# Twenty-six products in the last two groups: a negation leaves ScalarE, a raw quarter is derived by a sum, and the slab ring has eleven places

## The chip, the core and the metric

The kernel runs on one core of a Trainium2 chip. Its time is the device time of one execution in microseconds (us). A core has five engines that run beside each other, each with its own instructions in a fixed order: TensorE (PE; its weight loads are PEld) multiplies, VectorE (DVE), ScalarE (ACT) and GpSimd (POOL) work elementwise, and SyncE (SP) issues most transfers. A transfer that SP issues (SPq in the profile) waits in SP's order for what it depends on; everything behind it on SP waits too.

## The reference

Attention within chunks of 64 tokens is followed by a Fourier mix and a two-layer network, all in float32:

```python
# q, k, v: (8, 8, 576, 64); each chunk of 64 tokens attends to itself
attn = softmax(q_c @ k_c.T / sqrt(64)); x = (attn @ v_c)      # x: (8, 576, 512)
mixed = real(fft(fft(x, axis=1), axis=2))
u = x + mixed
un = (u - mean(u)) / sqrt(var(u) + 1e-6)                      # over the last axis
out = u + relu(un @ w_ch1) @ w_ch2                            # w_ch1: 512 x 2048, w_ch2: 2048 x 512
```

The change concerns the last product, with w_ch2, for the last two of nine groups of tokens.

## The kernel before, in words

**Groups and stages.** The tokens are cut into tiles of 128 and these into nine groups of four tiles (`groups`; eight groups of one batch entry each, and one of what is left of all). Each group passes an up stage (`un @ w_ch1` and relu, result `h1`) and a down stage (`h1 @ w_ch2` and the sum with u). While a group is multiplied, the attention and the Fourier mix of the next are done in between (`sides`), for the last groups no more. The generator `mlp(g)` yields after each small piece of TensorE work, and the loop at the end of the kernel hands out the other engines' work at each step `t`. The order on each engine is the order in which the Python code issues the instructions: nothing is rearranged.

**Fewer products.** From group 2 on the up stage (`up_halves`, L1271) and from group 1 on the down stage (`down_halves`, L1322) use seven half-size products in place of eight. For the last two groups (`FEW = NG - 2`, that is groups 7 and 8) the down stage is `down_few` (L1386): w_ch2 is seen as eight blocks b11 to b42, `h1` as sixteen blocks a11 to a44, and 26 products of sums of such blocks (`PRODUCTS`) give the result. A row of `PRODUCTS` names the left operand, the block on the right, a PSUM half (`c`, `b`, `d`, `f`, upper case for the second half), where the product is added with which sign (`+31` is block row 3, column 1), and the sums of `h1` blocks that GpSimd makes afterwards (`sums`, L1172). `EARLY` lists six such sums that are issued within the up stage of the same group, between products 15 and 20 of its 28.

**Blocks of w_ch2.** The right-hand blocks that are sums are made once, by `make_rest`, on GpSimd (L1122): `MADE` lists them, those whose name begins with s are stored in DRAM (`s3`, L1129). This is done in two halves of 512 columns each (`for half in range(2)`). A half first loads eight raw blocks from DRAM (`s2`, L1109), then makes 23 results: 22 on GpSimd, and `s18=-h` on ScalarE (L1118). They live in a list of 14 spare buffers of 128x512, taken from its front and given back at its end when the last reader has been issued; a buffer that is stored from is given back when the store has been issued, and the next writer waits for the store to land. A store is issued when three more stored blocks have been made after it. make_rest starts within the down stage of group 6 and is spread over the steps; at step `begin[FEW] + 2 * HF - 3`, late in the up stage of group 7, what is left of it is issued.

**The raw quarters.** w_ch2 as halves has four quarters. `keep2_whole` (L1079) and `keep2` (L1071) write three raw quarters and four sums to DRAM early in the program, for the seven products; `keep2_last` (L1083) writes the fourth raw quarter, the right half of the top rows (blocks b12 and b22), which only make_rest and the 26 products read.

**Slabs.** The right-hand operands come through rings of slabs in SBUF, filled by `fetch`: `fetch(1)` for the up stage (256 KB each, ten places, L1144, into `wa`), `fetch(2)` for seven-product down stages (1 MB, three places, L1149, into `wb`), `fetch(3)` for the 26 products (512 KB, six places, L1147, into `wb`). After each product one more slab is asked for, and waits for its place to be free. The first six `fetch(3)` are issued at the step named above, right after the rest of make_rest.

**Outputs.** `store` writes a finished tile: L1027 on SP for tiles of one kind, L1036 on SP and ScalarE for another, L1030 to L1032 for the last group. L1027 writes 128 KB in the shape 2x32x512.

**ScalarE in the up stage.** In each pair of the up stage, ScalarE copies a product from PSUM (L1276), which VectorE and later TensorE steps wait for, and applies relu (L1285, L1288, L1291). `s18=-h` stands between these.

Of the kernel before, what the change touches and what calls it, by code (L numbers as in the profile page):

```python
# [8 lines left out]
FP32 = mybir.dt.float32  # L9
# [7 lines left out]
def kernel(  # L17
# [32 lines left out]
    nc = tc.nc  # L50
    B, H, S, D = q.shape
    DM = H * D
# [8 lines left out]
    KF = DFF // 128  # L61
    HM, HQ = DM // 2, DM // 4
# [4 lines left out]
    G = 2 * NM  # L67
# [4 lines left out]
    one_p = ctx.enter_context(tc.tile_pool(name="one", bufs=1))  # L72
# [6 lines left out]
    dram = ctx.enter_context(tc.tile_pool(name="dram", bufs=1, space=bass.MemoryType.DRAM))  # L79
# [23 lines left out]
    NO, HF = 7, KF // 2  # L103
    UP = (1, 0, 2, 3, 4, 6, 5)
    s1 = dram.tile([HF // 2, NO, 128, 2 * 2 * 128], FP32, name="s1")
    s2 = dram.tile([NO + 1, 128, HF * HM], FP32, name="s2")
    NS1, NS2, Z1, Z2 = 10, 3, 2 * 2 * 128, HF * HM
    slab1 = [wa[:, i * Z1:(i + 1) * Z1].rearrange("p (k r f) -> p k r f", r=2, k=2) for i in range(NS1)]
    slab2 = [wb[:, i * Z2:(i + 1) * Z2].rearrange("p (m e) -> p m e", m=HF) for i in range(NS2)]
# [9 lines left out]
    NH, Z3 = 2, 4 * HM  # L119
# [1 line left out]
        ("a41", "b11", "c", "+41", "a41=a22+a42 a22=a21-a22 a21=a41-a21"),  # L121
        ("a44", "b42", "b", "+42", "a44=a24+a44 a31=a21+a31"),
        ("y0", "s8", "d", "+12", ""),
        ("y3", "s21", "c", "+31+32+42", "y3=y3+a43"),
        ("y1", "s0", "d", "+11+21", "y1=a44-y1 y1=y1-a23 y0=a12-y0"),
        ("a22", "b22", "f", "-22", "a22=a32-a34 a32=a42-a32"),
        ("a23", "s19", "d", "+22", ""),
        ("a44", "s15", "b", "+41", ""),
        ("a31", "s10", "f", "+32", "a31=a42-a22 a13=a13+a14 a24=a24+a31 a14=a14+a34 a34=a13+a34 y2=a34+y2"),
        ("y1", "s3", "b", "-21-22", ""),  # L130
        ("y3", "b32", "f", "+42", "a43=a44+a43 a12=a41-a12 a12=a12+a13 y0=y0-a32"),
        ("a22", "b21", "C", "+31", ""),
# [9 lines left out]
        ("a14", "s6", "D", "", ""),  # L142
        ("y2", "s18", "F", "-32", ""),
        ("a12", "b21", "B", "-11", ""),
        ("y0", "b22", "D", "+12", ""),
        ("a33", "s23", "F", "-31", ""),
    )
    EARLY = "y0=a11-a13 a11=a11-a21 y1=y0-a21 y2=a31-a41 a31=a33-a31 y3=y2-a33"
    MADE = (
        "u=b41-b31", "s3=b31-b41", "s15=u-b42", "s7=u-b11", "s8=b12+b22", "s0=u-s8", "t=b32-b42", "s19=u+t",  # L150
        "v=b32-b31", "s10=b11-b12", "s23=v-s10", "s21=s10-b32", "s24=s10-b22", "w=b22-b21", "s22=w-s10",
        "s4=b42-b41", "s25=w+s4", "s1=b21-s4", "s17=b21+b41", "h=b12+b32", "s12=h-s17", "s6=b42-h", "s18=-h",
    )
    STORED = tuple(text.split("=")[0] for text in MADE if text[0] == "s")
    NR2, NS3 = len(PRODUCTS), 6
    s3 = dram.tile([len(STORED), 128, Z3], FP32, name="s3")
    slab3 = [wb[:, i * Z3:(i + 1) * Z3].rearrange("p (m e) -> p m e", m=4) for i in range(NS3)]

    def parsed(text):

        out_, rest = text.split("=")
        sub = "-" in rest
        a, b = rest.split("-" if sub else "+")
        return out_, a, b, ALU.subtract if sub else ALU.add
# [913 lines left out]
        for o, m0, e0 in ((0, m, 0), (4, HF + m, 0), (5, HF + m, HM)):  # L1078
            nc.sync.dma_start(out=to[o, :, m:m + 2], in_=w2[:, m0:m0 + 2, e0:e0 + HM])  # L1079

    def keep2_last(i):
        to = s2.rearrange("o p (m e) -> o p m e", m=HF)
        nc.sync.dma_start(out=to[NO, :, 2 * i:2 * i + 2], in_=w2[:, 2 * i:2 * i + 2, HM:DM])  # L1083

    def block_of(name):

        if name[0] == "s":
            return s3[STORED.index(name)]
        k, j = int(name[1]) - 1, int(name[2]) - 1
        o = ((0, NO), (4, 5))[k // 2][j]  # L1090
        return s2[o, :, k % 2 * Z3:(k % 2 + 1) * Z3]

    def make_rest():

        z, spare = Z3 // 2, []
        for i in range(4):
            spare.append(xall[:, 2 * G:2 * G + 4, :].rearrange("p a f -> p (a f)")[:, i * z:(i + 1) * z])
        for tag, n in (("q", 2), ("k", 2), ("zf", 2), ("two", 1), ("qT", 1), ("kT", 1), ("pT", 1)):  # L1100
            t = one_p.tile([128, n * z], FP32, tag=tag, name="part")
            spare += [t[:, i * z:(i + 1) * z] for i in range(n)]
        last = {x: i for i, text in enumerate(MADE) for x in text.replace("=", "-").replace("+", "-").split("-")}
        for half in range(2):
            part = slice(half * z, (half + 1) * z)
            where, behind = {}, []
            for name in ("b31", "b41", "b42", "b11", "b12", "b22", "b32", "b21"):
                where[name] = spare.pop(0)
                nc.sync.dma_start(out=where[name], in_=block_of(name)[:, part])  # L1109
                if half and name in ("b41", "b11", "b22"):  # L1110
                    yield
            yield
            for i, text in enumerate(MADE):
                name = text.split("=")[0]
                to = spare.pop(0)
                if "=-" in text:
                    used = [text.split("-")[1]]
                    nc.scalar.mul(to, where[used[0]], -1.0)  # L1118
                else:
                    name, *used, op = parsed(text)  # L1120
                    in0, in1 = (where[x] for x in used)
                    nc.gpsimd.tensor_tensor(out=to, in0=in0, in1=in1, op=op)  # L1122
                where[name] = to
                if name in STORED:
                    behind.append(name)
                done_with = [x for x in (*used, name) if last[x] == i]
                while behind and (len(behind) > 3 or i == len(MADE) - 1):
                    old = behind.pop(0)
                    nc.sync.dma_start(out=block_of(old)[:, part], in_=where[old])  # L1129
                    if last[old] <= i and old not in done_with:  # L1130
                        done_with.append(old)
                spare += [where[x] for x in done_with if x not in behind]
                if i % 2:
                    yield
# [283 lines left out]
    with tc.manual_schedule():  # L1418
# [22 lines left out]
        n_w = 2  # L1441
# [45 lines left out]
            for gen in gens:  # L1487
                yield from gen

        n_whole, n_last, late, rest_ = 0, 0, [], None  # L1490
        conv2, conv1 = chain(conv2), chain(conv1)
        t = 0
        for g in range(NG):
            for _ in mlp(g):
                t += 1
                heavy = False
                for do in late:
                    do()
                late = []
                if t == 8:  # L1500
                    nc.scalar.copy(tk, early_tk[:, :, :, 0:NE])
                if cur < len(sides):
                    t0 = 3 if cur == 0 else ready_at[cur - 1]
                    t1 = ready_at[cur]
                    due = min(sizes[cur], (t - t0) * sizes[cur] // (t1 - t0))
                    while done < due:
                        heavy = next(sides[cur], None) or heavy
                        done += 1
                    if t >= t1:
                        for _ in sides[cur]:  # L1510
                            pass
                        cur, done = cur + 1, 0
                if not heavy:
                    round_next(late if t < KF and t % 4 == 3 else None)
# [12 lines left out]
                while n_last < HF // 2 and n_w > KF + 2 * n_last + 2:  # L1527
                    keep2_last(n_last)
                    n_last += 1
                if t == ready_at[FEW - 1]:  # L1530
                    rest_ = make_rest()
                    next(rest_)
                if t > ready_at[FEW - 1] + 4:
                    for _ in range(1 + t % 2):
                        next(rest_, None)
                if t == begin[FEW] + 2 * HF - 3:
                    for _ in rest_:
                        pass
                    for _ in range(NS3):
                        fetch(3)  # L1540
                if begin[1] <= t < begin[1] + KF // 2:
                    for _ in range(3):
                        next(conv1, None)
                if t == begin[1] + KF // 2:
                    for _ in range(NS2):
                        fetch(2)
                if t == begin[1] + KF:
                    for _ in range(NS1):
                        fetch(1)
# [49 lines left out]
```

## Time and profile before

| What | us |
|---|---|
| Three runs | 1097.26, 1098.84, 1100.13; median 1098.84 |
| The profiled execution's own time | 1097.62 |
| Its span, first to last instruction | 1095.6 |
| PE busy in the span | 1053.6 (96%) |
| DVE, ACT, POOL busy | 583.5, 310.4, 421.7 |
| Down stage of group 6 ends, up stage of group 7 begins | 878.4 |
| Up stage of group 7 ends, its down stage (26 products) begins | 948.5 |
| Down stage of group 7 ends | 996.2 |
| Up stage of group 8 | 996.2 to 1044.5 |
| Down stage of group 8 | 1044.5 to 1090.6 |

Times within the execution count from the first instruction. The groups of the profile show one sum of 128x512 on POOL (L1122) at about 1.27 us, a matmul of L1386 at 380 ns with the next one starting some 216 ns after it, and 52 loads of 512 KB `wb<-s` (the 26 products' slabs, twice). The mean TensorE clock that was granted is 0.990 of full speed; it is 0.91 from 880 to 900 us and 0.69 from 920 to 940 us, where TensorE is busy for 15.72 and 6.36 of 20 us. From 900 to 920 us the transfers moved 352 GB/s with the DMA engines fully busy. A bracket at the end of a timeline's line gives the idle time of the engine before it and what ended it; "SPq" and "ACTq" lines are the issue of transfers, with the time that the issue took.

### The profile page before, as it was taken

How to read it: one execution, taken by the hardware profiler on the slowest of the kernel's cores; microseconds unless marked ns; L12 is line 12 of the kernel's file. 1: busy time of each engine (PE TensorE's matmuls, PEld its weight loads, DVE VectorE, ACT ScalarE, POOL GpSimd, SP SyncE). 2: the span in 40 equal slices, each digit the busy share in tenths (PEclk: the TensorE clock that was granted, in tenths of full speed). 3: DMA queues.
4: the chain of work that ended last, by engine and by line, in shares of the span. 5: the costliest groups of instructions: out<-in, count | busy, mean ns of one | idle time of the engine just before them, and what ended most of it. 6: DMA issues, size and time to landing. Idle time of an engine off the chain costs nothing.

```text
span 1095.6 us, 19948 instructions
## 1 busy us (share of the span) xinstructions
PE 1053.6 (96%) x7386; PEld 836.7 (76%) x7386; DVE 583.5 (53%) x1273; ACT 310.4 (28%) x730; POOL 421.7 (38%) x539
## 2 busy tenths in 40 slices
PE   8999989999999999999999999999999987799997
PEld 6645544447888888888888888888888876688886
DVE  4898975325556456654565556545655422234331
ACT  4687653222113311332133103330223012101200
POOL 4311017564416140435133502541344659660281
PEclk9999999999999999999999999999999999899999
DMA  8767566598568445974676368936644478797366
GB/s 172 229 197 214 150 185 210 166 311 262 171 193 229 159 149 161 255 192 147 184 227 195 123 184 226 242 114 193 214 135 149 148 239 310 289 318 245 109 223 200
DMA packets 162829, 219.53 MB, mean 200 GB/s; under 512 B 69644, under 2 KB 107532, under 8 KB 157358
## 3 DMA queue, kind: packets, MB, share of 16 engines
q1 hardware_dynamic: 159084, 214.86, 64.0%
q10 hardware_dynamic: 3330, 2.76, 1.0%
q8 instruction: 59, 0.97, 0.4%
q0 software_dynamic: 320, 0.66, 0.3%
q14 instruction: 36, 0.29, 0.1%
HBM read 183.61 MB, written 34.60 MB: 199 GB/s over the span
## 4 chain that ended last, share of the span: by engine, by line
PE 70%; DMA 9%; POOL 6%; DVE 5%; issue 3%; ACT 3%; SPq 3%; DVEq 0%; POOLq 0%; ACTq 0%
PE pa L1271 15%; PE pb L1322 14%; PE pa L1322 11%; PE pb L1271 11%; PE dn L1386 7%; PE up L1204 2%; POOL part L1122 2%; PE pt L397 2%; DMA xall<-in_moe_w_ch_dram 2%; DMA wb<-s 2%; DMA s<-part 2%; PE mix L838 2%; PE z L719 1%; PE xp L498 1%; SPq L263 1%
## 5 line engine op out<-in xcount | busy, mean ns | idle before, releaser
L1271 PE MATMUL pa<-unT,wa 128*128 128x256 f32 x672 | 161.7, 384 | 5.0 <-ACT h L1285 3.4
L1271 PEld LDWEIGHTS pa<-unT,wa 128*128 128x128 f32 x672 | 127.3, 192 | 23.6 <-ACT h L1285 3.8
L1271 PE MATMUL pb<-wa 128*128 128x256 f32 x448 | 106.6, 381 | 0.0
L1271 PEld LDWEIGHTS pb<-wa 128*128 128x128 f32 x448 | 84.5, 190 | 11.6
L1322 PE MATMUL pa<-wb,h 128*128 128x256 f32 x384 | 87.2, 380 | 0.0
L1322 PE MATMUL pb<-wb,h 128*128 128x256 f32 x384 | 86.4, 379 | 0.0
L1322 PEld LDWEIGHTS pa<-wb,h 128*128 128x128 f32 x384 | 71.8, 190 | 9.7
L1322 PEld LDWEIGHTS pb<-wb,h 128*128 128x128 f32 x384 | 72.0, 190 | 9.3
L1158 POOL TENSOR_TENSOR h<-h 128x256 f32<-128x256 f32 x48 | 41.0, 864 | 94.0 <-DVE wb L1156 91.2
L555 POOL COPY xall<-xall 1x512 f32<-1x512 f32 x28 | 17.8, 636 | 147.9 <-DVE xall L515 120.5
L1271 PE MATMUL pa<-wa 128*128 128x256 f32 x224 | 55.4, 392 | 14.6 <-ACT wa L1276 14.6
L1386 PE MATMUL dn<-wb,h 128*128 128x256 f32 x304 | 67.9, 380 | 1.5 <-DMA wb<-s 1.5
L1277 DVE TENSOR_TENSOR wa<-pb,wa 128x256 f32<-128x256 f32 x56 | 23.6, 425 | 84.4 <-ACT wa L1276 84.4
L1386 PEld LDWEIGHTS dn<-wb,h 128*128 128x128 f32 x304 | 57.2, 190 | 9.8 <-DVE wb L1396 2.2
L1271 PEld LDWEIGHTS pa<-wa 128*128 128x128 f32 x224 | 42.6, 194 | 21.8 <-ACT wa L1276 15.4
L1225 PE MATMUL dn<-wb,h 128*128 128x512 f32 x128 | 58.4, 605 | 0.0
L1204 PE MATMUL up<-unT,wa 128*128 128x512 f32 x128 | 56.8, 595 | 0.0
L1172 POOL TENSOR_TENSOR h<-h 128x512 f32<-128x512 f32 x36 | 45.1, 1267 | 27.4 <-ACT h L1291 23.4
L1276 ACT COPY wa<-pa 128x256 f32<-128x256 f32 x56 | 20.6, 372 | 119.7 <-PE pa L1271 92.9
L1271 PE MATMUL pb<-unT,wa 128*128 128x256 f32 x224 | 52.9, 379 | 0.0
L1184 PE MATMUL up<-unT,wa 128*128 128x512 f32 x108 | 49.4, 598 | 0.0
L1285 ACT ACTIVATE h<-pa 128x256 f32<-128x256 f32 x56 | 21.3, 383 | 97.1 <-PE pa L1271 96.6
(284 smaller groups left out, 2005.5 us busy)
## 6 DMA issues: line engine op xcount, KB each, us to landing
wa<-s SPq DMA_DIRECT2D x196, 256.0 KB
wb<-s SPq DMA_DIRECT2D x42, 1024.0 KB
wb<-s SPq DMA_DIRECT2D x52, 512.0 KB
xall<-in_moe_w_ch_dram SPq DMA_DIRECT2D x22, 512.0 KB
q<-in_q_dram SPq DMA_DIRECT2D x96, 112.0 KB
k<-in_k_dram SPq DMA_DIRECT2D x96, 112.0 KB
v<-in_v_dram SPq DMA_DIRECT2D x124, 64.0 KB
s<-part SPq DMA_DIRECT2D x27, 256.0 KB
```

Source lines behind the costliest of these rows:

```text
L397: nc.tensor.transpose(pt[:, j, :], src(j), ident)
L838: nc.tensor.matmul(out=mix[:, cols], lhsT=zt[:, T], rhs=tab, start=(T == 0), stop=(T == 3), skip_group_check=True,)
L1122: nc.gpsimd.tensor_tensor(out=to, in0=in0, in1=in1, op=op)
L1158: nc.gpsimd.tensor_tensor(out=h1[:, m, hi], in0=h1[:, m, lo], in1=h1[:, m, hi], op=ALU.subtract)
L1172: nc.gpsimd.tensor_tensor(out=out_, in0=a, in1=b, op=op)
L1184: nc.tensor.matmul(out=up, lhsT=w1[:, kk, m * 128:(m + 1) * 128], rhs=unT[:, kk], start=(kk == 0), stop=(kk == KD - 1), skip_group_check=True,
L1204: nc.tensor.matmul(out=up, lhsT=w1[:, kk, m * 128:(m + 1) * 128], rhs=unT[:, kk], start=(kk == 0), stop=(kk == KD - 1),)
L1225: nc.tensor.matmul(out=dn, lhsT=h1[:, m, s * 128:(s + 1) * 128], rhs=w2[:, m, :], start=(m == 0), stop=(m == KF - 1),)
L1271: nc.tensor.matmul(out=dst, lhsT=w[:, kk, r], rhs=rhs[o][:, kk], start=(o in (0, 1) and kk == 0), stop=(kk == 1), skip_group_check=True,)
L1277: nc.vector.tensor_tensor(out=b, in0=pbs[r][:, 0], in1=a, op=ALU.add)
L1322: nc.tensor.matmul(out=dst, lhsT=lhs[:, m], rhs=w[:, m], start=(o in (0, 2) and m == 0), stop=(m == HF - 1), skip_group_check=True,)
L1386: nc.tensor.matmul(out=dst, lhsT=lhs[:, m], rhs=w[:, m], start=(fresh and not half and m == 0), stop=(m == 3), skip_group_check=True,)
```

## The change

- Names `d` and `w` are added to the blocks that make_rest loads: they are the two halves of a sum that `keep2` stores already (`s2[2]`, the right quarter minus the left quarter of the top rows). `b12` is made as `d + b11` and `b22` as `w + b21`; the latter is stored under the name `sb22`. The fourth raw quarter (`keep2_last`, four transfers of 256 KB) is no longer written.
- `s18` is `b12 + b32`, without the sign that ScalarE gave it; `s21` has the opposite sign. The signs go into sums of `h1` blocks (`EARLY`, two rows of `PRODUCTS`).
- `MADE` is in another order. All of its 23 entries a half are made by GpSimd; 19 of them are stored, where it was 18.
- The ring for the 26 products has eleven places: the six in `wb`, two in the rows of `xall` and three in the buffers tagged q, k and zf, which make_rest used as spares. Eleven `fetch(3)` are issued where six were.

The diff, without the unchanged rows and the removed counter `n_last`:

```diff
-        ("y3", "s21", "c", "+31+32+42", "y3=y3+a43"),
+        ("y3", "s21", "c", "+31+32+42", "y3=a43-y3"),
-        ("a22", "b22", "f", "-22", "a22=a32-a34 a32=a42-a32"),
+        ("a22", "sb22", "f", "-22", "a22=a32-a34 a32=a42-a32"),
-        ("a31", "s10", "f", "+32", "... a34=a13+a34 y2=a34+y2"),
+        ("a31", "s10", "f", "+32", "... a34=a13+a34 y2=y2-a34"),
-        ("y0", "b22", "D", "+12", ""),
+        ("y0", "sb22", "D", "+12", ""),
-    EARLY = "y0=a11-a13 a11=a11-a21 y1=y0-a21 y2=a31-a41 a31=a33-a31 y3=y2-a33"
+    EARLY = "y0=a11-a13 a11=a11-a21 y1=y0-a21 y2=a41-a31 a31=a33-a31 y3=y2+a33"
     MADE = (
-        "u=b41-b31", "s3=b31-b41", "s15=u-b42", "s7=u-b11", "s8=b12+b22", "s0=u-s8", "t=b32-b42", "s19=u+t",
-        "v=b32-b31", "s10=b11-b12", "s23=v-s10", "s21=s10-b32", "s24=s10-b22", "w=b22-b21", "s22=w-s10",
-        "s4=b42-b41", "s25=w+s4", "s1=b21-s4", "s17=b21+b41", "h=b12+b32", "s12=h-s17", "s6=b42-h", "s18=-h",
+        "u=b41-b31", "s3=b31-b41", "s15=u-b42", "s7=u-b11", "t=b32-b42", "s19=u+t", "v=b32-b31", "s4=b42-b41",
+        "b12=d+b11", "s10=b11-b12", "s23=v-s10", "s21=b32-s10", "sb22=w+b21", "s8=b12+sb22", "s0=u-s8",
+        "s24=s10-sb22", "s22=w-s10", "s25=w+s4", "s1=b21-s4", "s17=b21+b41", "s18=b12+b32", "s12=s18-s17", "s6=b42-s18",
     )
-    NR2, NS3 = len(PRODUCTS), 6
+    NR2, NS3 = len(PRODUCTS), 11
-    slab3 = [wb[:, i * Z3:(i + 1) * Z3].rearrange("p (m e) -> p m e", m=4) for i in range(NS3)]
+    slab3 = [wb[:, i * Z3:(i + 1) * Z3].rearrange("p (m e) -> p m e", m=4) for i in range(6)]
-    def keep2_last(i):
-        to = s2.rearrange("o p (m e) -> o p m e", m=HF)
-        nc.sync.dma_start(out=to[NO, :, 2 * i:2 * i + 2], in_=w2[:, 2 * i:2 * i + 2, HM:DM])
     def make_rest():
...
-            for name in ("b31", "b41", "b42", "b11", "b12", "b22", "b32", "b21"):
+            for name in ("b31", "b41", "b42", "b11", "b32", "d", "w", "b21"):
...
-                if "=-" in text:
-                    used = [text.split("-")[1]]
-                    nc.scalar.mul(to, where[used[0]], -1.0)
-                else:
-                    name, *used, op = parsed(text)
-                    in0, in1 = (where[x] for x in used)
-                    nc.gpsimd.tensor_tensor(out=to, in0=in0, in1=in1, op=op)
+                name, *used, op = parsed(text)
+                in0, in1 = (where[x] for x in used)
+                nc.gpsimd.tensor_tensor(out=to, in0=in0, in1=in1, op=op)
...
-                while n_last < HF // 2 and n_w > KF + 2 * n_last + 2:
-                    keep2_last(n_last)
-                    n_last += 1
...
                 if t == begin[FEW] + 2 * HF - 3:
                     for _ in rest_:
                         pass
+                    more = [xall[:, 2 * G:2 * G + 4, :].rearrange("p a f -> p (a f)")[:, i * Z3:(i + 1) * Z3] for i in range(2)]
+                    more += [one_p.tile([128, Z3], FP32, tag=tag, name="more") for tag in ("q", "k", "zf")]
+                    slab3.extend(a.rearrange("p (m e) -> p m e", m=4) for a in more)
                     for _ in range(NS3):
                         fetch(3)
```

More of the change, by code (lines that the diff above doesn't have):

```diff
@@ L105 @@
     s1 = dram.tile([HF // 2, NO, 128, 2 * 2 * 128], FP32, name="s1")
-    s2 = dram.tile([NO + 1, 128, HF * HM], FP32, name="s2")
+    s2 = dram.tile([NO, 128, HF * HM], FP32, name="s2")
     NS1, NS2, Z1, Z2 = 10, 3, 2 * 2 * 128, HF * HM
@@ L123 @@
         ("y0", "s8", "d", "+12", ""),
-        ("y3", "s21", "c", "+31+32+42", "y3=y3+a43"),
+        ("y3", "s21", "c", "+31+32+42", "y3=a43-y3"),
         ("y1", "s0", "d", "+11+21", "y1=a44-y1 y1=y1-a23 y0=a12-y0"),
-        ("a22", "b22", "f", "-22", "a22=a32-a34 a32=a42-a32"),
+        ("a22", "sb22", "f", "-22", "a22=a32-a34 a32=a42-a32"),
         ("a23", "s19", "d", "+22", ""),
         ("a44", "s15", "b", "+41", ""),
-        ("a31", "s10", "f", "+32", "a31=a42-a22 a13=a13+a14 a24=a24+a31 a14=a14+a34 a34=a13+a34 y2=a34+y2"),
+        ("a31", "s10", "f", "+32", "a31=a42-a22 a13=a13+a14 a24=a24+a31 a14=a14+a34 a34=a13+a34 y2=y2-a34"),
         ("y1", "s3", "b", "-21-22", ""),
@@ L1088, in block_of @@
             return s3[STORED.index(name)]
-        k, j = int(name[1]) - 1, int(name[2]) - 1
-        o = ((0, NO), (4, 5))[k // 2][j]
-        return s2[o, :, k % 2 * Z3:(k % 2 + 1) * Z3]
+        o, k = (2, "dw".index(name)) if name in "dw" else ({"b1": 0, "b2": 0, "b3": 4 + "12".index(name[2]), "b4": 4 + "12".index(name[2])}[name[:2]], (int(name[1]) - 1) % 2)
+        return s2[o, :, k * Z3:(k + 1) * Z3]
     def make_rest():
@@ L1106, in make_rest @@
             where, behind = {}, []
-            for name in ("b31", "b41", "b42", "b11", "b12", "b22", "b32", "b21"):
+            for name in ("b31", "b41", "b42", "b11", "b32", "d", "w", "b21"):
                 where[name] = spare.pop(0)
                 nc.sync.dma_start(out=where[name], in_=block_of(name)[:, part])
-                if half and name in ("b41", "b11", "b22"):
+                if half and name in ("b41", "b11", "d"):
                     yield
@@ L1488, in chain @@
                 yield from gen
-        n_whole, n_last, late, rest_ = 0, 0, [], None
+        n_whole, late, rest_ = 0, [], None
         conv2, conv1 = chain(conv2), chain(conv1)
```

## The prediction

> **What bounds the kernel now.** TensorE is busy for 96% of the span, so a gain can only come where it stands still. I read the waits of TensorE from 860 us on first (columns: us in total, times, longest):
>
> ```profile
> PE pa L1271 <- ACT wa L1276: 14.6, 2, 13.6
> PE pa L1271 <- ACT h L1285: 3.4, 1, 3.4
> PE dn L1386 <- DMA wb<-s: 1.5, 2, 0.7
> ```
>
> Nearly all of it lies in the up stage of group 7 (878.4 to 948.5 us), and the releaser is ScalarE. The chain of waits from 860 to 960 us says who held ScalarE (start, length, what):
>
> ```profile
> 869.53 0.53 SPq L1027
> ...
> 870.73 9.11 DMA s<-part
> ...
> 895.25 6.40 DMA s<-part
> ...
> 902.03 6.24 DMA part<-s
> ...
> 937.47 0.63 ACT part L1118
> 938.10 0.27 ACT wa L1276
> 938.41 3.38 PE pa L1271 x8
> ```
>
> Between the lines left out stands GpSimd (POOL L1122), without a break from 904.5 to 937.5. The negation L1118 waits for GpSimd's late sum h; the copy L1276, which TensorE needs, is queued behind it. The timelines of GpSimd and of SP's queue show what paces GpSimd:
>
> ```profile
> 879.97 1.26 POOL L1122 TENSOR_TENSOR part<-part 128x512 f32<-128x512 f32 x1 [11.54 <-DMA s<-part]
> ...
> 893.81 1.26 POOL L1122 TENSOR_TENSOR part<-xall,part 128x512 f32<-128x512 f32 x1
> ...
> 904.48 2.50 POOL L1122 TENSOR_TENSOR part<-part 128x512 f32<-128x512 f32 x2 [9.41 <-DMA part<-s]
> ...
> 938.75 1.26 POOL L1122 TENSOR_TENSOR xall<-xall,part 128x512 f32<-128x512 f32 x1
> ```
>
> ```profile
> 884.73 2.29 SPq L1036 DMA_DIRECT2D out_dram<-wb  x2
> 889.42 0.34 SPq L1129 DMA_DIRECT2D s<-xall  x1
> ...
> 941.88 3.00 SPq L1147 DMA_DIRECT2D wb<-s  x6
> ```
>
> GpSimd waits 11.54 us for a buffer whose store stood on SP behind an output (L1027), then 9.41 us for the second half's loads, and ends its last sum at 940.0. Only then, at 941.88, does SP ask for the first slab of the down stage, because the program puts `fetch(3)` behind all of make_rest. So two things end within some us of each other: the up stage, held by ScalarE (948.5), and the slabs, held by GpSimd (by 948.5 at the latest, since TensorE goes from L1271 to L1386 without a wait).
>
> **The Trainium skill.** "DMA: Bandwidth & Descriptors", section "Why a DMA increments its semaphore by 16 and not by 1": a transfer runs on the largest number of engines, up to 16, that divides the slowest dimension of both patterns. The output L1027 starts with a dimension of 2, so on two. The trace agrees in effect: the store behind it took 9.11 us, another at 908.65 took 4.79. "TensorE: Matmul & The Clock Gate", Part 1: after an idle window of about 3.4 us the array runs at half clock until busy again for about as long. Here the eight matmuls after the 13.64 us gap took 3.38 us, where eight follow the next at 1.73. "GPSIMD Engine Reference", section 3.1, gives about 2.6 cycles an element, at the page's 1.2 GHz an estimate of 1.11 us for 512; the trace has 1.26 us for a 128x512 sum, which is used.
>
> **Part by part.**
>
> *The negation.* Two ScalarE instructions of 0.63 us go, and with them the queueing. The up stage has 28 turns of 1.727 us (group 8: 996.16 to 1044.51 is 48.35), and took 70.1: 21.7 were lost, 17.9 as waits, the rest at half clock. Without it group 7's up stage could end at 878.4 + 48.4 + 0.9 (a wait at 882 that stays) = 927.7. Some of its slab loads (L1144) stand on SP behind stores that wait for GpSimd: I expect up to 3 us, so about 930. What is late next is the first down slab.
>
> *GpSimd.* Each half now has 23 sums on it instead of 22, and one more stored block. I walked the list of spare buffers and the built program's order. First half: in both kernels GpSimd halts for the first store behind L1027, which lands at 879.9; before, ten sums were done by then, after, only nine (s15's store has moved behind L1027). So 14 sums remain instead of 12: 14 x 1.26 = 17.6, to 897.6 (before 895.1). A new wait: s24 goes into the buffer that s23 is stored from. It is due at 887.5; s23 is issued at about 882.5, behind the second pair of outputs (879.90 to 881.00), one of which SP still waited for at 889.4. Before, the buffer of s23 was rewritten at 891.25 without idle time, so it had landed by then. Bounds 0 and 3.7; I take landing at 890.6, a wait of 3.1. First half ends at 900.7. Queued behind this wait are all other sums and, on SP, their stores and the slab loads behind those.
>
> *Turn-around to the second half.* Before 9.4 us, with a backlog of stores. Now GpSimd's pace has thinned the stores; the nearest row for one transfer is the 4.79 us above. Bounds 4.8 and 9.4, I take 5.0: start at 905.7 (before 904.5). Second half: 23 sums and, by the order of the built program, all six EARLY sums stand before the last one (before: 22 and five): 29 x 1.26 = 36.5, plus 0.3 for a store (before 1.5): end at 942.5, before 940.0.
>
> *First slab.* In the built program one store and two slab loads lie between the last sum and `fetch(3)`: 1.5 us, so 944.0. It lands behind 0.77 MB: with its own 0.52 MB, 1.29 MB at the 352 GB/s of 900 to 920 us are 3.7, and 0.9 to start: 4.6 (bounds 3.5, and 6.6, the most it can have taken before). The down stage starts at 948.6, before at 948.5: **+0.1**. The 18 us between 930 and 948.6 hold the freed time. After such a gap half clock costs 3.38 - 1.73 = **+1.65** (bounds 0 and 1.7).
>
> *Eleven slabs.* Group 7's down stage took 47.63; 26 x 1.727 and four turns of 0.44 are 46.66: **-0.97**. In group 8 the last slab is asked for behind the outputs L1030:
>
> ```profile
> 1084.10 0.35 SPq L1147 DMA_DIRECT2D wb<-s  x1
> ...
> 1088.59 1.97 PE L1386 MATMUL dn<-wb,h 128*128 128x256 f32 x8 [0.73 <-DMA wb<-s]
> ```
>
> The product before it starts at 1085.97, so this one could start at 1087.70: **-0.89**; with eleven slabs this load is issued ahead of all L1030. Five more slabs asked for at once (2.6 MB) delay the next group's L1144 loads, which have the whole down stage as cover. A slab takes 1.5 us at 352 GB/s, less than a product's 1.73.
>
> *Raw quarter.* Four stores of 256 KB at 105 to 134 us go. There SP waits for VectorE's weight rounding before nearly every load, so they are hidden: **-0.3** (bounds -1.6, their issue time, and +0.5). The turned signs in EARLY and PRODUCTS change no instruction's cost.
>
> Sum: 0.1 + 1.65 - 0.97 - 0.89 - 0.3 = -0.4 us, on the profiled execution's own 1097.62 (span 1095.6 and 2.0 around it): 1097.2. The median of the three runs, 1098.84, is 1.2 above it: **1098.4**.
>
> **The rivals.** *The stall passes through:* the down stage starts at 927.7, 20.8 earlier and without half clock: -20.8 - 0.97 - 0.89 - 0.3 = -23.0, 1075.9. For it: the releaser is ScalarE. Against: fetch(3) behind make_rest. *A quick chain:* s23's store has landed when s24 is due; 3.1 less, -3.5 in all, 1095.3. For it: DMA is busy for 0.4 of 880 to 884. Against: SP's own wait at 889.4. *A slow turn-around, slower than before:* the second half's loads take 9.4 us again, because slab loads delayed by the stores come at the same moment; +4.4, so +4.0, 1102.8. It decides from a turn-around of 8.7 us on. For it: that is what before shows. Against: fewer transfers are under way. *The ring is deep in name only:* SP's transfers count on eight semaphores in turn, so a ninth waits for the first; the last wait stays, 1099.3.
>
> **How the numbers follow.** Forecast 0.49, ring in name only 0.04 (both within 0.3%, which is 3.3 us, about what a measurement of this kernel can tell from no change), quick chain 0.21, pass-through 0.04, slow turn-around 0.22. Faster by over 0.3%: 0.25; within: 0.53; slower: 0.22. The range is 1094.0 to 1103.5: it takes in the quick chain with a slab landing 1.1 earlier, and the slow turn-around; the pass-through and the corners where bounds add up are left out. The forecast's own range is 1096 to 1101.
>
> **What would show it.** Right: no ScalarE wait at L1276 but 0.9 us; the up stage of group 7 over by 933; then a wait of some 18 us at the first `dn`, released by DMA; the GpSimd idle times at 880 (11 to 14 us), 887 (3 us) and 901 (5 us); its last sum at 942 to 943; no wait before the last product. Wrong: a first `dn` before 945 or after 952, or waits of TensorE on slabs inside a down stage.

## The result, and the profile after

| | before | changed |
|---|---|---|
| Median | 1098.42 us (7 runs, 1097.26 to 1100.13) | 1105.67 us (7 runs, 1101.74 to 1108.25) |
| Ratio | 1 | 1.0058, 95% interval 1.0040 to 1.0076 |
| Profiled execution: own time, span | 1097.62, 1095.6 | 1106.11, 1104.2 |

The change makes the kernel slower by 0.58%; 1098.4 us was forecast. The stages of the two profiled executions add up to the difference of the spans (us; start and length of each):

| Stage | before | changed | difference |
|---|---|---|---|
| up stage of group 7 begins | 878.42 | 876.38 | -2.04 |
| its length, with the wait behind it | 70.11 | 73.59 | +3.48 |
| down stage of group 7 | 47.63 | 48.30 | +0.67 |
| up stage of group 8 | 48.35 | 55.13 | **+6.78** |
| down stage of group 8, to the last product's start | 44.08 | 43.17 | -0.91 |
| from there to the end of the span | 7.0 | 7.6 | +0.6 |

In kernel.py of the changed kernel the sums are L1113, their stores L1120, their loads L1104, the slabs of the up stage L1135 and those of the 26 products L1138. The waits of TensorE from 860 us on, in the changed kernel (us in total, times, longest):

```profile
PE dn L1377 <- DMA wb<-s: 17.6, 1, 17.6
PE pb L1262 <- DMA wa<-s: 7.8, 3, 4.0
PE pa L1262 <- ACT wa L1267: 0.9, 1, 0.9
```

The waits on ScalarE are gone but for 0.9 us. In their place stands one wait of 17.6 us for the first slab of group 7's down stage, as predicted, and a new row, three waits on `wa` slabs (two in group 7's up stage, one in group 8's). The timeline of GpSimd has the halts in its brackets:

```profile
875.48 1.27 POOL L1113 TENSOR_TENSOR part<-xall 128x512 f32<-128x512 f32 x1 [12.12 <-DMA s<-part]
...
886.55 2.51 POOL L1113 TENSOR_TENSOR part<-part 128x512 f32<-128x512 f32 x2 [3.31 <-DMA s<-part]
...
903.03 1.26 POOL L1113 TENSOR_TENSOR part<-part 128x512 f32<-128x512 f32 x1 [6.50 <-DMA part<-s]
...
914.17 1.26 POOL L1113 TENSOR_TENSOR xall<-part 128x512 f32<-128x512 f32 x1 [2.27 <-DMA s<-xall]
```

And the chain of waits shows what starts the down stage of group 7 (start, length, what):

```profile
940.70 1.23 POOL part L1113
...
941.94 0.32 SPq L1120
...
943.29 6.54 DMA wb<-s
949.84 0.14 issue
949.97 10.22 PE dn L1377 x39
```

The last sum, one store, two slab loads, the first `fetch(3)` at 943.29 and its landing: this is the path of the prediction. The last product of the kernel has no bracket any more:

```profile
1096.57 1.89 PE L1377 MATMUL dn<-xall,h 128*128 128x256 f32 x8
```

What the prediction doesn't have is in the up stage of group 8. TensorE's timeline there:

```profile
1013.81 1.89 PE L1262 MATMUL pa<-wa 128*128 128x256 f32 x8
1019.73 3.75 PE L1262 MATMUL pb<-unT,wa 128*128 128x256 f32 x8 [4.03 <-DMA wa<-s]
1023.27 2.66 PE L1262 MATMUL pa<-unT,wa 128*128 128x256 f32 x8
1025.77 1.89 PE L1262 MATMUL pb<-wa 128*128 128x256 f32 x8
```

The wait of 4.03 us is for the eleventh slab of this stage, the first that is asked for within the stage. The turn that needs it starts 5.92 us after the one before it instead of 1.73, the next two 3.54 and 2.50 us later, at reduced clock (0.50 of full speed from 1020 to 1024 us): 4.19 + 1.81 + 0.77 = 6.77, the whole 6.78. Why the slab is late is on SP's queue:

```profile
973.13 12.11 SPq L1138 DMA_DIRECT2D wb<-s  x5
985.33 0.85 SPq L1036 DMA_DIRECT2D out_dram<-wb  x2
986.28 0.37 SPq L1138 DMA_DIRECT2D wb<-s  x1
986.75 7.75 SPq L1138 DMA_DIRECT2D xall<-s  x2
994.59 0.84 SPq L1036 DMA_DIRECT2D out_dram<-wb  x2
995.55 1.63 SPq L1138 DMA_DIRECT2D more<-s  x3
...
1009.61 2.41 SPq L1135 DMA_DIRECT2D wa<-s  x4
```

SP needs 12.11 us for five issues and 7.75 us for two. The first load of `wa` goes out at 1009.61, 11.3 us after the stage began (before: 5.4). The ring's ten places cover ten turns, 17.3 us, so 5.9 us are left for a landing that takes 10.0. In the kernel before this landing took 10.9 us: of the cover of 17.3 us, 16.3 were used already, and only 1.0 was in hand.

What SP waits for in the changed kernel from 942 to 1020 us:

```profile
SPq L1138 <- DMA out_dram<-wb: 14.6, 2, 7.6
SPq L1138 <- DMA wb<-s: 7.8, 7, 1.9
```

The longest wait of the same queue in the kernel before, from 940 to 1020 us:

```profile
SPq L1147 <- PE dn L1386: 24.0, 19, 2.1
```

Before, the slab loads wait for products, and for no output. Now two of them wait 7.6 and 7.0 us for the landing of an output, which has nothing to do with their data. The link is a semaphore, a counter (called a count below) that a transfer raises by 16 as it lands. In the trace the transfers of SP and of ScalarE use the same eight (numbers 101 and 103 to 109 in its instructions), and SP waits for the earlier transfer on a semaphore to land before it issues the next one on it. The load issued at 984.44 uses semaphore 109, as ScalarE's output of 982.50 did, and that output landed at 984.38; the load at 994.18 uses 107, as ScalarE's output of 988.12 did, which landed at 994.12. These outputs are finished by the seventeenth and the twentieth product, while the two loads follow the fifteenth and the nineteenth. What SP could not ask for in time it then asks for at once: six slabs from 994.2 to 997.8, which land 3.6 to 8.8 us later. Two outputs L1027 wait until 1001.7 and 1002.9 for such landings, and the second of them and the last slab take 3.5 and 3.0 us to issue; only then comes `wa`.

Why the slab needs ten us to land can be read from its semaphore too: 14 of its 16 steps had come by 1013.9, in time for the turn due at 1015.5, the last two at 1019.4 and 1019.6. The four outputs L1027, issued from 998.5 to 1002.9 and put on two DMA engines by the prediction, raise theirs in one step at once and two late ones, the last at 1017.7. So the slab, too, stands behind these outputs on two engines. This is read from the times; no run here gave L1027 another shape.

### The profile page after: what moved, and what is told of

It is laid out like the page before. It is cut to its first block, busy times and chain, and to the rows that moved or that the text cites. A ratio compares the mean times of both kernels' runs of the same rounds, so it can differ in the third digit from the quotient of the medians.

```text
span 1104.2 us, 19936 instructions
## 1 busy us (share of the span) xinstructions
PE 1055.9 (96%) x7386; PEld 838.0 (76%) x7386; DVE 580.5 (53%) x1273; ACT 310.1 (28%) x728; POOL 423.9 (38%) x541
## 4 chain that ended last, share of the span: by engine, by line
PE 72%; DMA 9%; POOL 5%; DVE 4%; SPq 3%; ACT 3%; issue 2%; DVEq 0%; POOLq 0%; ACTq 0%
PE pa L1262 15%; PE pb L1313 14%; PE pb L1262 12%; PE pa L1313 11%; PE dn L1377 8%; DMA xall<-in_moe_w_ch_dram 2%; PE pt L397 2%; PE up L1195 2%; PE mix L838 1%; PE z L719 1%; SPq L263 1%; POOL part L1113 1%; DMA v<-in_v_dram 1%; PE xp L498 1%; PE up L1175 1%
## 5 line engine op out<-in xcount | busy, mean ns | idle before, releaser
L1262 PEld LDWEIGHTS pb<-wa 128*128 128x128 f32 x448 | 84.2, 190 | 13.7 <-issue 2.2
L1262 PE MATMUL pb<-unT,wa 128*128 128x256 f32 x224 | 55.9, 395 | 6.0 <-DMA wa<-s 6.0
L1377 PE MATMUL dn<-wb,h 128*128 128x256 f32 x176 | 41.4, 390 | 17.6 <-DMA wb<-s 17.6
L1267 ACT COPY wa<-pa 128x256 f32<-128x256 f32 x56 | 20.8, 372 | 123.3 <-PE pa L1262 97.3
L1262 PEld LDWEIGHTS pb<-unT,wa 128*128 128x128 f32 x224 | 44.1, 198 | 13.0 <-issue 6.7
L1377 PEld LDWEIGHTS dn<-wb,h 128*128 128x128 f32 x176 | 34.3, 197 | 22.7 <-issue 18.0
```

The lines of the kernel that those rows point to most:

```text
L1262: nc.tensor.matmul(out=dst, lhsT=w[:, kk, r], rhs=rhs[o][:, kk], start=(o in (0, 1) and kk == 0), stop=(kk == 1), skip_group_check=True,)
L1267: nc.scalar.copy(a, dst)
L1377: nc.tensor.matmul(out=dst, lhsT=lhs[:, m], rhs=w[:, m], start=(fresh and not half and m == 0), stop=(m == 3), skip_group_check=True,)
```

## The experiments

Two theories stood after this. A: transfers of SP and of ScalarE count on the same eight semaphores; with eleven places two slab loads of SP come to stand behind outputs that ScalarE issues later. B: five more slabs asked for at once are 2.6 MB more to move, and `wa` comes late whoever issues what. And the start of the down stage had its own: C, it hangs on GpSimd's chain, because `fetch(3)` stands behind it.

**e1: the changed kernel with six places.**

```diff
-    NR2, NS3 = len(PRODUCTS), 11
+    NR2, NS3 = len(PRODUCTS), 6
...
-                    more = [...]
-                    slab3.extend(...)
```

> The changed kernel with its ring of six slabs, all else as changed. If the ring's eleven places cost the 6.8 us in group 8's up stage (48.35 us before, 55.13 after), this stage takes 48.4 to 49 us again, with no wait of TensorE on wa inside it; group 7's down stage gets back a wait on slabs of some 0.7 to 1.0 us, and the wait of 0.7 before the last product comes back, of which the end of the outputs gives back most: in all -5.5 us, about 1100 us. If the stall in the up stage comes from the later stores and loads of GpSimd's sums instead, it stays, and the time stays at 1105 to 1106 us. The down stage of group 7 starts at 949 to 950 us either way.

Measured: 1100.71 us, ratio to the kernel before 1.0018 (1.0007 to 1.0029). Group 8's up stage takes 48.35 us, without a wait; group 7's down stage 48.60; the wait before the last product is back (0.67 us). So the stall goes with the ring: 1.0058 against 1.0018 are 4.4 us by the ratios (5.0 by the medians).

**e2: eleven places, group 7's outputs all on SP.**

```diff
-                    eng = nc.scalar if r else nc.sync
+                    eng = nc.scalar if r and n not in groups[FEW] else nc.sync
```

> The changed kernel with eleven slabs, but group 7's outputs are all issued by SP, none by ScalarE. Theory A (completion counts taken in turn by both issuing engines: a slab load on SP waits for the landing of an output that ScalarE issues only after a later product): SP's waits on out_dram in group 7's down stage (2, 14.6 us) go, the DMA engines don't fall to 0.6 of 980 to 996 us, the loads of wa start by 1003 us instead of 1009.6, group 8's up stage takes 48.4 to 49.5 us: -5 to -7 us, about 1100 us. Theory B (five slabs more are 2.6 MB more for the DMA engines to move, whoever issues what): the up stage stays at 54 to 56 us and the time at 1105 to 1107 us.

Measured: 1100.92 us, 1.0010 (0.9994 to 1.0025). The up stage of group 8 takes 48.35 us. SP's longest rows from 940 to 1020 us:

```profile
SPq L1138 <- PE dn L1377: 15.8, 13, 1.8
SPq L1120 <- POOL part L1113: 7.5, 5, 3.4
```

The slab loads L1138 wait for products again and for no output (the `wa` loads L1135 wait 4.4 us for outputs, as they do in the kernel before). The bytes are the same, and so theory B falls as the cause of the stall. The windows of both kernels at the same distance from the down stage's start (it begins 3.55 us later in e2; columns: window, length, busy us of PE, PEld, DVE, ACT, POOL with counts, clock, DMA share, GB/s), first the changed kernel, then e2:

```profile
964.00:980.00 16.00, 16.00 (x80) 14.09 (x79) 6.77 (x15) 0.59 (x1) 15.69 (x13) 1.00 1.03 420
980.00:996.00 16.00, 16.00 (x80) 14.09 (x79) 6.52 (x16) 0.59 (x1) 0.40 (x1) 1.00 0.61 203
```

```profile
968.00:984.00 16.00, 16.00 (x80) 14.10 (x79) 7.34 (x15) 0.59 (x1) 15.33 (x13) 1.00 1.03 420
984.00:1000.00 16.00, 16.00 (x80) 14.09 (x79) 6.15 (x15) 0.59 (x1) 0.54 (x1) 1.00 0.91 319
```

B has this much truth: with eleven places the DMA engines are full until 980 us. They would have caught up in the next 16 us, but in the changed kernel they stand idle for 0.39 of it, since SP asks for nothing. In e2 the first `wa` load goes out 5.2 us into the stage.

**e3: the kernel before, with eleven places alone.** The five places are made as in the change; negation, fourth quarter and sums stay.

> The kernel before with the ring of eleven alone: negation, fourth raw quarter and sums as they were. If the ring alone brings the stall in group 8's up stage, that stage takes 53 to 56 us, group 7's down stage 46.7 us (no half clock there, since TensorE doesn't stand still ahead of it; no waits on slabs), the last wait goes: 1098.4 + 6.8 - 1.0 - 0.2 = 1104 us. If the stall needs the other parts of the change too, the stage takes 48.4 us and the time is 1097 us.

Measured: 1103.62 us, 1.0049 (1.0035 to 1.0063): the ring alone makes the kernel before 5.4 us slower. Group 7's down stage takes 46.65 us, group 8's up stage 51.92. The waits of TensorE on `wa`, and SP's waits:

```profile
PE pb L1271 <- DMA wa<-s: 3.3, 1, 3.3
```

```profile
SPq L1147 <- DMA out_dram<-wb: 13.8, 2, 7.4
```

The same two waits on outputs as in the changed kernel. The stall needs none of the other parts.

**e4: the kernel before, without the negation alone.**

```diff
-        "h=b12+b32", "s12=h-s17", "s6=b42-h", "s18=-h",
+        "s18=b12+b32", "s12=s18-s17", "s6=b42-s18",
```

The signs of y2, y3 and s21 are turned as in the change.

> The kernel before with the negation alone taken out (h is stored as it is, the signs of y2, y3 and s21 turned), ring of six, fourth quarter stored as before. My theory: group 7's up stage ends at 928 to 931 us without the waits on ScalarE, and TensorE then waits for the first slab, whose load stands behind GpSimd's last sum (end at 938 to 940): the down stage starts at 945.5 to 948.5 (before 948.5), and pays 1.65 us at half clock: 1096.5 to 1100 us, 1098 the likeliest. Rival: the stall passes through to the end, 1076 to 1080 us.

Measured: 1099.02 us, 1.0005 (0.9994 to 1.0015): no difference that can be told. The waits on ScalarE are gone, and the down stage starts 70.34 us after the up stage's start, before 70.11. Its chain of waits:

```profile
941.44 1.23 POOL part L1122
...
944.52 5.63 DMA wb<-s
950.15 0.14 issue
950.28 9.85 PE dn L1386 x32
```

So 18 us of waiting on ScalarE were taken away, and TensorE waits 18.3 us for a slab instead: theory C. The products behind this gap then lose 2.8 us to the clock (sixteen matmuls take 6.40 us, 3.62 in the kernel before).

**e5 and e6: group 6's outputs on ScalarE.** GpSimd's halt of 12.1 us is a wait for a store that stands on SP behind L1027. SP's queue in the changed kernel:

```profile
855.38 0.38 SPq L1120 DMA_DIRECT2D s<-part  x1
866.30 1.10 SPq L1027 DMA_DIRECT2D out_dram<-wb  x2
867.50 1.91 SPq L1120 DMA_DIRECT2D s<-part  x2
```

SP waits for the output's data from 855.8 to 866.3 with sums already made behind it. e5 (six places) and e6 (eleven, group 7's outputs on SP as in e2) take these outputs off SP:

```diff
-                nc.sync.dma_start(out=to, in_=o[r0:r0 + CH])
+                (nc.scalar if n in groups[FEW - 1] else nc.sync).dma_start(out=to, in_=o[r0:r0 + CH])
...
-                    eng = nc.scalar if r else nc.sync
+                    eng = nc.scalar if r or n in groups[FEW - 1] else nc.sync
```

The last line is that of e5; in e6 it also keeps group 7's outputs on SP.

> The changed kernel with ring of six, and group 6's outputs all issued by ScalarE, so that the stores of GpSimd's sums on SP don't stand behind them. Theory: the start of group 7's down stage is set by GpSimd's chain, and that by the halts of 12.1 us and 3.3 us for stores behind these outputs. Without them the first half of the sums ends at 881 to 884 us (896.5), the second starts at 888 to 891 (903.0), the last sum ends at 925 to 929 (941.9), the first slab is asked for at 927 to 931 (943.3); the first product starts at 932 to 936 us (950), and as the gap before it is short there is no half clock: -15 to -19 us, 1082 to 1086 us. Rival: the outputs hold up ScalarE's copies in the next up stage, or the second half's loads collide with the slab loads of the up stage, which then stalls: 1090 to 1098 us. Rival of the sums: the gain is 12 us at most because the halt for the second store comes at another buffer.

> The same with the ring of eleven and group 7's outputs all issued by SP, so that neither issuing engine waits for the other's outputs. The first product of group 7 starts at 932 to 936 us as with six; no waits on slabs inside the down stages; the loads into the five added places wait for the last stores out of them, which is behind the first six loads. 1081 to 1085 us, 0.5 to 1 us less than with six. If the eleven slabs at once delay wa after all, now that the down stage begins as soon as the up stage ends, group 8's up stage takes 51 to 55 us and the time is 1085 to 1090 us.

Measured: e5 1096.59 us, 0.9985 (0.9972 to 0.9999); e6 1096.99 us, 0.9983 (0.9973 to 0.9992). Both are a little faster than the kernel before, some 3 us better than e1 and e2 without the move (1.0018 and 1.0010), where 15 to 19 us were expected. In e6 GpSimd's timeline has these halts:

```profile
863.34 1.27 POOL L1113 TENSOR_TENSOR part<-xall 128x512 f32<-128x512 f32 x1 [1.18 <-DMA s<-part]
901.88 1.26 POOL L1113 TENSOR_TENSOR part<-part 128x512 f32<-128x512 f32 x1 [16.89 <-DMA part<-s]
912.43 1.27 POOL L1113 TENSOR_TENSOR xall<-part 128x512 f32<-128x512 f32 x1 [1.66 <-DMA s<-xall]
```

The halts of 12.1 and 3.3 us are gone, the first half of the sums ends at 885, and then GpSimd waits 16.9 us for the second half's loads. The gain was given back at the next wait. These loads stand on SP behind four `wa` loads, which wait for places that TensorE frees one in 1.73 us. But SP waits for something else too, in e6 from 874 to 902 us:

```profile
SPq L1135 <- DMA out_dram<-wb: 7.5, 2, 7.3
SPq L1120 <- DMA out_dram<-wb: 6.2, 2, 3.5
SPq L1135 <- PE pa L1262: 1.2, 2, 0.8
```

For 13.7 us (11.7 in e5) it stands with `wa` loads and stores that wait for the landing of outputs which ScalarE now issues: the shared semaphores again, though e6 was built so that neither issuing engine waits for the other's outputs. (The store of 890.37 uses 108, as ScalarE's output of 881.53 did; that landed at 890.3.) Much of this runs beside the wait for places: the fourth `wa` load went out at 892.3, when its place had been free since 889.0. So by these times some 3 us of the 16.9 come from the outputs, the rest from the order on SP. The time of e5 lies in the range of its first rival, but in neither run does TensorE wait for a `wa` slab.

**e7: two raw slabs early.** On e2, the first two `fetch(3)`, of b11 and b42, which no sum makes:

```diff
+                if t == begin[FEW] + 4:
+                    for _ in range(2):
+                        fetch(3)
...
-                    for _ in range(NS3):
+                    for _ in range(NS3 - 2):
```

> The changed kernel with eleven slabs and group 7's outputs on SP, and the first two slabs of group 7 (raw quarters b11 and b42, which wait for no sum) asked for early in its up stage instead of behind the last sum; the other nine where they were. Theory (the first slab's load behind GpSimd's chain sets the start): two products (3.5 us) run right after the up stage, at 930 to 934 us, and the third waits for s8's slab until 948.5 to 952 us; the time falls by 2.5 to 4 us against 1100.9, to 1097 to 1098.5 us. Rival: another thing than that load holds TensorE at the start of the down stage (a sum of GpSimd for the first products): nothing is gained, 1100 to 1102 us.

Measured: 1097.41 us, 0.9986 (0.9975 to 0.9997), 3.5 us under e2 in the medians and 2.6 by the ratios. The first product starts at 934.11, the third waits 12.9 us for s8's slab. Two products of 1.73 us moved from behind the gap to before it: theory C again, and no wait but that for the slab held the start.

**e8: the second half's loads sooner.** On e6, make_rest's steps are handed out faster up to these loads, and slower behind them:

```diff
-                    for _ in range(1 + t % 2):
+                    for _ in range(2 if t < begin[FEW] + 3 else 1):
                         next(rest_, None)
```

> As e6 (eleven slabs, group 6's outputs on ScalarE, group 7's on SP), and make_rest takes two steps a turn of the program until the second half's loads are issued, then one, so that these loads no longer stand on SP behind slab loads (L1135) that wait for TensorE. Theory: in e6 GpSimd stood still for 16.9 us before the second half because of that place in SP's order. Now the loads are issued at 882 to 887 us, the second half starts at 888 to 892 (901.9), the last sum ends at 925 to 930, the first product of group 7 starts at 930 to 936 us (947.9), with a gap before it of 0 to 6 us: -12 to -17 us and little or no half clock, 1080 to 1085 us. Rival: the second half's loads and stores push the wa loads of group 7's up stage back, TensorE stalls inside it, and the down stage starts at 940 to 947: 1089 to 1096 us.

Measured: 1091.59 us, 0.9926 (0.9902 to 0.9950). This lies in its rival's range, but the cause is another: TensorE waits for no `wa` slab, it waits 7.5 us for ScalarE's copy L1267 at the start of group 7's up stage, as in e9 below (the profiled execution, at 1097.28 us, is the longest of the six).

**e9** is e8 with e7's two slabs early:

> The same with the two raw slabs asked for early in the up stage, as in e7. The first two products follow the up stage without a gap, the third waits for s8's slab, which is asked for behind the last sum: up to 3.5 us less than e8, 1078 to 1083 us. If e8's down stage already starts less than 3.5 us behind its up stage, the gain is only what that gap was; if the early loads (1 MB) delay the second half's loads, e9 is slower than e8 by 1 to 3 us.

Measured: 1087.34 us, 0.9895 (0.9872 to 0.9918): 12 us under the kernel before and the lowest median here (its interval and e8's overlap a little), but 4 us over what was expected. The second half started at 895.0, not 890, and a wait of 5.9 us on ScalarE stands in group 7's up stage. ScalarE's timeline in e9:

```profile
871.77 1.71 ACTq L1027 DMA_DIRECT2D out_dram<-wb  x2
881.90 3.17 ACTq L1036 DMA_DIRECT2D out_dram<-wb  x4
886.42 1.39 ACTq L1027 DMA_DIRECT2D out_dram<-wb  x2
887.90 3.46 ACTq L1036 DMA_DIRECT2D out_dram<-wb  x4
891.45 0.65 ACT L1267 COPY wa<-pa 128x256 f32<-128x256 f32 x2 [28.19 <-DMA out_dram<-wb]
```

The first L1036 goes out at 881.90, in e6 at 873.60. Behind the outputs stands the copy L1267, and behind that TensorE. This is the trap of the ring, turned round, and the trace's semaphores show it: the output of 881.90 uses semaphore 108, as a store that SP issued at 875.24 did, which landed at 881.82; the last one, at 891.03, uses 107, as a load that SP issued at 886.30 did, which landed at 891.01. In e6 the output of 873.60 follows a store of 867.46, which had landed at 869.4.

**e10: outputs held.** e9, but group 6's outputs stay on SP and are issued one tile a step behind the second half's loads:

```diff
+        if n in groups[FEW - 1] and not now:
+            held.append((n, o))
+            return
...
+                if held and t >= begin[FEW] + 3:
+                    store(*held.pop(0), now=True)
```

> As e9, but group 6's outputs don't go to ScalarE: they are held back and issued on SP one tile at a time behind the second half's loads, when their data have long been made. In e9 ScalarE's outputs waited until 881.9 us for counts that SP's stores of GpSimd's sums held, and its copy L1267 stood behind them until 891.5: TensorE waited 5.9 us and ran at half clock. Theory: this wait goes, the up stage of group 7 ends 6 to 9 us sooner against its start; the third product then waits for s8's slab for 1 to 6 us; in all 3 to 7 us less than e9, 1080 to 1084 us. Rival: held outputs, slow to land, take counts that the stores and slab loads behind them on SP need, and the second half starts or ends later: 1086 to 1092 us.

Measured: 1091.63 us, 0.9944 (0.9926 to 0.9961); slower than e9. The wait on ScalarE is gone and the first product starts at 931.23 (e9: 938.97), but the third waits 8.6 us. GpSimd now halts behind transfers that come late, the last time an output (in e10 the sums are L1118):

```profile
904.69 1.27 POOL L1118 TENSOR_TENSOR xall<-part 128x512 f32<-128x512 f32 x1 [5.42 <-DMA s<-xall]
910.45 1.27 POOL L1118 TENSOR_TENSOR part<-xall,part 128x512 f32<-128x512 f32 x1 [3.27 <-DMA s<-part]
916.95 1.27 POOL L1118 TENSOR_TENSOR part<-part,xall 128x512 f32<-128x512 f32 x1 [2.65 <-DMA out_dram<-wb]
```

Its rival had such halts. They use up a start of the second half that is 4.6 us earlier than in e9 (890.4), and the last sum ends at 938.5 as in e9 (938.6). So the third product starts at 943.46, in e9 at 943.79: theory C once more. Behind its longer gap (8.6 us against 1.2) the next 24 matmuls take 8.12 us, in e9 5.42; this is about the 2.6 us between the two profiled executions.

## Why the prediction was wrong

*The step that failed* is in "Eleven slabs": "Five more slabs asked for at once (2.6 MB) delay the next group's L1144 loads, which have the whole down stage as cover." Two things are wrong in it. The cover is not the down stage: ten slabs of the next up stage are loaded already in the stage before, the other eighteen are asked for one at a time within that up stage, and each has ten turns, 17.3 us, of which the kernel before used 16.3. And the delay is not a matter of bytes: e2 moves the same bytes without a stall. The prediction knew that a transfer waits for an earlier one on its semaphore, and used it only for a rival in which the ring does nothing ("deep in name only"); it counted SP's transfers alone. ScalarE's outputs take their turn too. In the profile with six places (e1) ScalarE's two outputs of a tile take their counts next to SP's two of the same tile; with eleven places five of SP's slab loads have their counts between them. So a load that stands ahead of SP's own output in the queue comes to follow ScalarE's on its count, and waits for an output that isn't due, with all of SP behind it. Why the built program deals the counts in that order with eleven places is open. The delay was put at nothing, and the ring as a whole at -1.86 (-0.97 and -0.89). The ring alone measured +5.4 us on the kernel before (e3) and +4.4 on the changed one (e1). With the outputs on SP it comes to 1.0010 (e2) against 1.0018 (e1), 0.9 us less, which the two intervals don't tell apart.

*The negation: right.* The stall ended as a wait for the first slab: up stage over at 932.4 (predicted "by 933"), a wait of 17.6 (some 18). e4 shows it alone: no gain.

*GpSimd: right in its places, short in its sizes.* The halts came as named, 12.1 (11 to 14), 3.31 (3.1 taken), but the turn-around was 6.50 and not 5.0, a store cost 2.27 and not 0.3, and the first slab landed in 6.54 instead of 4.6: 1.5 + 2.0 + 1.9 = 5.4 us, against which the chain began 4.4 us sooner (the first halt ended at 875.5, predicted 879.9). That the two nearly cancel is luck. The 0.9 us "to start" in the term for the first slab had no measured row behind it. These are scatter as much as error: e1 and e2 have the same sums, stores and loads up to this point and show turn-arounds of 6.04 and 7.13, and first products 70.67 and 73.34 us after the up stage's start (changed: 73.59, predicted 70.2). So the +3.48 of the table belongs only in part to the change, and so does the -2.04: up stages of group 7 began between 876.4 and 880.4 us in these six profiles, and nothing in the change was shown to move that.

*Half clock: right for this run, by luck.* +1.65 predicted; 48.30 - 46.66 = 1.64. But 1.7 was too narrow a bound: after like gaps e2 lost 2.5 us, e4 2.8 and e5 3.1. The Trainium skill, "TensorE: Matmul & The Clock Gate", Part 1, has the array at half clock for about as long as the window of 3.4 us, which makes an estimate of half of that, 1.7 us, for the loss; e5's loss is 1.8 times as much. The clock that the traces record shows where the spread comes from. Its spells at half speed last 3.41, 6.83, 10.24, 13.65, 17.07 or 20.48 us (but for the one cut off by the end), which are one to six times 3.41. They end on such steps, and the first product falls anywhere between two. Half speed lasted for 3.2 us after its start in the changed kernel, 4.9 in e2, 5.5 in e4 and 6.1 in e5; half of these are 1.6, 2.4, 2.7 and 3.0 us, the losses.

*Eleven slabs, the gains themselves: right.* No slab wait in either down stage, no wait before the last product (-0.91). But of that, 0.6 us came back behind it: SP issues the last outputs at about 1.13 us a triple whether the product is early or not.

*The sum without the ring* can be checked: 0.1 + 1.65 - 0.3 = +1.45 us for the rest of the change; e1 measured +0.18%, 2.0 us (0.8 to 3.2). The rest was priced right in sum, though by terms whose errors cancel; the ring was not.

*The rivals.* Pass-through: refuted by e4. The quick chain didn't come (its halt was 3.31 us), nor did a turn-around of 9.4 us (6.50). The loss came from a place that no rival named; "deep in name only" had the semaphores, but not ScalarE's share in them.

What stays open: why the counts fall as they do, what L1027 in a shape for more engines would bring, and whether the part of the change that gets a raw quarter back by a sum costs anything by itself (e1 against e4, 1.0018 and 1.0005, overlap).

## What to carry to other kernels

A deeper ring is free only if its loads can be issued: before adding places, list every transfer that shares the queue and the completion counts, those of other engines too, and ask of each which later event it waits for. Moving an output to another issuing engine doesn't take it out of this list. When a stall is taken away, follow the work to the next in-order queue: here 18 us of ScalarE waits turned into 18 us of slab waits, 15 us of GpSimd halts into 17 us of waiting for loads, and only several steps together (e9) brought 12 us. And say for each transfer how long its own cover is, from the turn that asks for it to the turn that reads it, and how much of it is used already.

## What was not expected of the hardware

Outputs from two issuing engines share one set of completion semaphores in the built program: a slab load on SP stood 7.6 us for an output of ScalarE that was 64 KB and no data of its own.

The outputs L1027 raise their semaphores in three steps, and transfers behind them get the last two of their sixteen steps late: 5.7 us after the others for the first `wa` slab of group 8 in the changed kernel, 6.4 in the kernel before. The store of 9.11 us in the prediction's chain is another: 14 steps by 875.7, the last two at 878.7 and 879.8.

The loss to the clock after a gap of 16 to 18 us was 1.6, 2.5, 2.8 and 3.1 us in four profiles (changed, e2, e4, e5), for sixteen matmuls of the same shape. A gap of 3.6 us (e8) cost 2.8 us as well, one of 1.2 us (e9) less than 0.1.

And the same instructions (changed, e1, e2) put the first product of the down stage up to 2.9 us apart against the start of the up stage. Between changed and e1, 2.4 us of this lie in GpSimd's waits for transfers (24.2 us against 21.8).
